# The same FFT and two MLP blocks with the engines' work listed in another order

## The chip, the cores and the metric

The kernel runs on one core of one Trainium2 chip. A core has five engines that work side by side, each through its own instructions in their order: TensorE (PE) does the matmuls, VectorE (DVE), ScalarE (ACT) and GpSimd (POOL) work elementwise, and SyncE (SP) issues most of the transfers. The metric is the device time of one execution in microseconds, as the median of several runs.

## The reference

The input x (2 batches of 3008 rows of 256) goes through three stages:

```python
X = np.fft.fft(x, axis=1)
X = np.fft.fft(X, axis=2)
x = X.real.reshape(6016, 256)
h = x @ w_in                                   # 256 -> 2048
x = (h * np.clip(h + 3.0, 0.0, 6.0) / 6.0) @ w_out
xn = x / np.sqrt(np.mean(x * x, -1, keepdims=True) + 1e-06) * rms_g
g = xn @ w_gate                                # 256 -> 1536
out = (g / (1.0 + np.exp(-g)) * (xn @ w_val)) @ w_out2
```

## The kernel before

All tensors of 32-bit numbers are split into a high and a low word that TensorE takes, so each product is three matmuls (high x high, high x low, low x high). The low word is made by a subtraction, `sub` at L271 to L272, on GpSimd or on VectorE. The weights come as 64-bit words and are decoded on the chip: `decode` (L254) is one ScalarE instruction (L260) and four of VectorE (L262, L263, L265, L267), then a copy for the high word and a `sub` for the low one.

The Fourier transform along the rows is done as matmuls with cosine and sine matrices (L439, from `smm`), after the input has been folded by symmetry (`sums`, `fold`). Its even and odd halves are added and subtracted into the arrays PQ and X (L456 to L461 and L469 to L478; the last three lines are copies of X by DMA). The transform along the 256 columns is multiplied into the first weights: `wmm` (L302) multiplies the columns' matrices by a quarter of w_in at L309, and splits the result at L318 and L320 into the array A0 to A3. One row of the product is copied out (L313), stored to memory as row0 to row3 (L315), and loaded again in another layout as c_wx (L322).

Phase 1 has 96 items, one for 1004 columns of tokens and 128 hidden channels (`item1`): six matmuls into the banks E and O (L536), a VectorE instruction that adds the x128 part by c_wx (L540), a sum and a difference (L542, L543), the activation (L548 on ScalarE, L551 on VectorE), the high word (L554), the low word (L272) and 12 matmuls into four acc banks (L570). E and O exist twice, so an item's first matmuls need that L551 two items back is done. Phase 2 has 144 items of 502 tokens (`item2`): 12 matmuls into E and O (L693), sigmoid (L696), two products (L699, L701), the high word (L705), the low word (L272), and six matmuls into two acc banks (L715). `rms` (L631) makes one normalized block of tokens from the results of phase 1, for 12 items each: a square on ScalarE, a sum over the channels by two matmuls (L649) into one of the E banks, a reciprocal square root in three rounds between ScalarE and VectorE (L654 to L664), a product (L667) and a split into words (L670, L672). `load_w2` and `conv_w2` bring and decode the weights of phase 2 while phase 1 runs.

What sets the order is a list written as a string, STEPS: 2554 words, each the name of a task in the table TASKS, a plain number for an item of phase 1, or a number with + for one of phase 2. Each word lets that task go on to its next `yield`, and everything it issues on the way is put at the end of the engines' queues:

```python
low[0] = V if step != task else G
```

A word with an apostrophe puts its subtraction L272 on VectorE, one without puts it on GpSimd. An engine does its instructions in that order alone; semaphores make it wait for what an instruction needs. So a step that stands early can hold up all that is queued behind it on each engine that it uses.

Of the kernel before, what the change touches and what calls it, by code (L numbers as in the profile page):

```python
# [83 lines left out]
    mat12 dwo0 PQ111 mat12 pq00' dwo0 PQ012 mat12 dwo0' ev01 PQ112 ev01 dwi1 lwo1 0 ev11 dwi1 ev11 dwi1 1 0 sx1 dwi1 sx1
    sx1 0 dwi1 X10 1 0 dwi1 1 X11 lwi2 0 1 X12 lwi3 lwo3 wt1 0 1 pq01 0 2 evx1 1 0 evx1 wt1 dwo1 2 1 2 0 wt1 1 wt1 wt1
    dwo1 2 evx1 pq01 dwi3 2 1 dwi3 2 wt1 wt1 2 lwo2 3 g wt1 wt1 2 3 4 dwi3 2 3 dwi3 3 4 3 4 5 3 dwo1 3 4 5 4 3 5 6 4 dwo1
    4 5 3 6 dwo1 5 4 6 7 5 dwo1 6 7 7 5 4 dwi2 6 5 dwi2 7 8 dwi2 6 5 7 6 dwi2 6 9 8 7 8 7 6 9 8 7 9 8 9 7 8 9 dwi2 8 10 9
    8 7 11 10 9 10 9 8 11 10 dwi2 11 10 11 9 dwo2 11 10 dwo2 10 wt2 11 dwo2 12 10 g wt2 12 11 12 10 wt2 dwi3 11 wt2 wt2
# [10 lines left out]
    45 pq10' 47 45 46 44 47 45 46 ls01 47 46 45 47 46 47 46 48 46 47 gr01 48 47 48 46 47 48 46 lm12 gr01 48 ls11 gr01 49
    48 48 47 49 49 48 ls11' 49 50 lw00 47 49 50 gr11 49 50 49 50 49 48 50 cw00 gr11 cw00 gr11 51 50 cw00 cw00 pq11 50 52  # L100
    51 lw10 cw00 lw01 51 50 49 52 51 cw00 52 51 52 50 51 52 51 53 52 51 54 53 52 53 51 52 54 53 54 53 54 52 53 54 rms2 53
    55 54 rms2 53 56 55 55 pq11 53 56 55 56 54 cw01 55 54 cw01 57 55 56 55 54 57 56 55 57 58 56 cw01 57 cw01 56 55 58 lw11
    cw01 57 56 cw01' 59 57 58 cw10 57 56 59 58 cw10 57 59 58 57 59 cw10 58 59 58 60 cw10 59 58 61 lw20 cw10 60 60 cw10 58
    61 60 59 cw10 61 cw11 59 60 59 61 cw11 60 cw11 61 60 62 cw11 61 60 lw21 cw11 63 62 62 61 60 63 cw11 62 63 61 cw20 cw11
    62 61 63 cw20 62 cw20 63 62 64 cw20 63 62 cw20 65 64 64 63 62 65 cw20 64 65 63 cw21 cw20 64 63 65 cw21 64 cw21 65 64
    66 63 cw21 64 67 66 65 66 64 cw21 65 67 66 67 65 rms0 66 cw21 65 67 66 cw21 67 66 rms0 68 67 66 69 68 68 67 66 69 67
    68 69 68 69 67 68 69 68 70 69 68 71 70 69 70 68 69 71 70 71 70 71 69 70 71 rms0 70 rms0 72 71 70 73 72 72 71 70 73 71
    72 73 72 73 71 72 73 72 rms0 73 74 72 rms0 75 rms0 73 74 rms0 72 74 73 75 74 rms0 75 73 rms0 75 74 rms0 75 74 76 pq12
    rms0 74 77 76 75 76 74 77 75 74 76 77 75 76 pq12 77 78 76 77 75 rms1 76 78 78 76 79 rms1 77 rms0 78 77 76 79 rms0 79
    77 78 79 77 rms0 78 79 78 rms0 80 79 78 rms0 81 79 80 78 81 79 80 81 80 79 rms0 81 80 lw30 rms0 81 80 82 rms0 79 80 83  # L110
    82 82 cw30 80 81 83 80 82 cw30 81 83 81 82 cw30 81 83 cw30 82 lw40 83 82 84 83 82 85 84 83 84 82 83 85 84 85 84 85 83
    84 85 84 86 85 84 87 86 85 86 84 cw30 85 87 86 cw30' 87 85 86 87 86 87 86 88 87 86 rms1 89 88 88 tw1 86 87 89 88 87 89
    88 89 87 88 89 88 rms1 90 89 88 91 90 90 tw2 88 89 91 90 89 91 90 91 89 90 91 90 rms1 91 92 90 rms1 93 rms1 91 92 90
    92 91 93 92 93 91 92 93 92 93 92 94 93 92 95 94 94 93 92 95 93 94 95 94 95 93 94 95 rms1 94 rms1 +0 95 94 rms1 95 94
    +0 rms1 +0 95 +0 rms1 +1 +0 rms1 +0 rms1 rms1 95 rms1 +1 rms1 rms1 +1 lw31 rms1 +2 +1 95 rms1 +1 +3 +2 +1 cw31 +2 cw31
    +2 +0 cw31 +2 +3 cw31 +2 +4 +3 lw41 cw31 +3 cw31 +3 +3 cw40 +5 +4 cw40 +4 cw40 +4 +1 +5 cw40 +4 +5 lw50 cw40 +6 +4 +5
    +5 cw40 +5 +2 +6 cw41 +6 +7 cw41 +6 cw41 +6 cw41 +6 +3 lw51 +7 cw41 +7 +4 cw41' +7 +8 +7 cw50 +7 cw50 +9 cw50 +8 cw50
    +8 lw60 cw50 +8 cw50 +5 +8 +9 +8 cw51 +9 +10 cw51 +9 cw51 +9 cw51 +9 +6 +10 lw61 cw51 +10 +11 cw51 +10 +10 cw60 +10
    cw60 +12 +11 cw60 +11 cw60 +11 +7 lw70 cw60 +11 cw60 +12 +8 +12 +11 cw61 +12 +13 cw61 +12 cw61 +12 cw61 +9 +13 +13
    lw71 cw61 +14 +13 cw61 +13 cw70 +13 cw70 +10 +14 rms2 cw70 +15 +14 cw70 +14 lw80 cw70 rms2 +14 cw70' +11 +14 +15 cw71  # L120
    +15 +12 cw71 +15 rms2 cw71 +15 +13 rms2 cw71 +15 lw81 cw71 +14 cw71' cw80 +16 cw80 cw80 cw80 cw80 +15 +16 cw80' +16
    +17 cw81 +16 cw81 +16 cw81 +16 cw81 +18 +17 +17 cw81 +17 +16 cw81' +17 +18 +17 +19 +18 +18 +18 +18 +17 +19 +19 +20 +19
    rms2 +19 +19 +21 +20 +20 rms2 +20 rms2 +20 +18 rms2 +21 +20 +21 rms2 +22 +21 rms2 +21 rms2 +21 rms2 +23 +22 rms2 +22
# [725 lines left out]
```

## Time and profile before

| | |
|---|---|
| median of 3 runs | 1104.33 us (1103.52 to 1104.47) |
| profiled execution | 1106.04 us |
| its span | 1104.1 us |
| mean granted TensorE clock | 0.992 |
| TensorE busy | 1056.1 us, 96%, 4572 matmuls |
| VectorE / ScalarE / GpSimd busy | 774.9 / 537.5 / 501.0 us |

The span runs from the first instruction to the last. The table by stage cuts it at places where the work changes: the transform up to about 60 us, its remainder mixed with the first items to about 142, phase 1 to about 500 (with the second batch's transform in it up to 366), then phase 2. Its busy times stand in the order PE, PEld (the loading of weights into TensorE), DVE, ACT, POOL. "Idle before <-" behind a timeline row is the time for which that engine had nothing to do, and what ended it.

### The profile page before, as it was taken

Reading aid. Unit: us, or ns where it says so; the run is one execution under the profiler, and the core shown is the slowest. Engines: PE = TensorE matmul, PEld = TensorE weight load, DVE = VectorE, ACT = ScalarE, POOL = GpSimd, SP = SyncE. Lnnn points to the kernel's source line nnn. Section 1 sums busy time; section 2 is a strip of 40 time slices with the busy share of each in tenths; the row PEclk is TensorE's granted clock in tenths of the full one; section 3 lists DMA queues with packets and bytes.
Section 4 is the critical chain, followed back from the end, with each engine's and each line's share of the span. In section 5 each row is a group of like instructions: output and inputs, shape, how many; then the busy total and the mean of one; then the engine's idle time right before and its main releaser. Section 6 shows DMA issues by size and latency. Waiting matters only on the chain.

```text
span 1104.1 us, 12691 instructions
## 1 busy us (share of the span) xinstructions
PE 1056.1 (96%) x4572; PEld 865.2 (78%) x4572; DVE 774.9 (70%) x1173; ACT 537.5 (49%) x814; POOL 501.0 (45%) x384
## 2 busy tenths in 40 slices
...
PEclk9899999999999999999999999999999999999999
...
GB/s 294 136 173 1 80 12 65 1 83 47 129 7 96 39 0 20 39 39 44 109 58 20 19 1 20 2 17 19 1 19 1 19 8 12 19 1 20 1 19 20
DMA packets 19175, 47.21 MB, mean 43 GB/s; under 512 B 3942, under 2 KB 7014, under 8 KB 18478
## 3 DMA queue, kind: packets, MB, share of 16 engines
...
## 4 chain that ended last, share of the span: by engine, by line
PE 67%; DVE 19%; POOL 5%; issue 3%; ACT 3%; DMA 2%; SPq 0%; DVEq 0%; ACTq 0%; POOLq 0%
PE acc L715 16%; PE E L693 16%; PE O L693 16%; PE acc L570 12%; POOL LO L272 4%; PE E L536 3%; PE O L536 3%; DVE R L551 3%; DVE T L540 2%; DVE O L543 2%; DVE E L542 2%; ACT HI L554 1%; PE E L439 1%; PE O L439 1%; DMA J<-in_x 1%
## 5 line engine op out<-in xcount | busy, mean ns | idle before, releaser
L272 POOL TENSOR_TENSOR LO<-R,HI 128x502 fp32r<-128x502 f32 x192 | 260.9, 1387 | 143.9 <-ACT HI L554 143.9
L570 PE MATMUL acc<-HI,B 128*128 128x502 f32 x768 | 248.4, 392 | 0.0
L699 DVE TENSOR_TENSOR R<-T,E 128x502 f32<-128x502 f32 x144 | 97.2, 675 | 201.1 <-ACT T L696 187.7
L272 POOL TENSOR_TENSOR HI<-R,HI 128x502 fp32r<-128x502 f32 x87 | 116.6, 1340 | 231.7 <-ACT HI L705 231.5
L570 PEld LDWEIGHTS acc<-HI,B 128*128 128x128 f32 x768 | 145.4, 189 | 30.6 <-POOL B L272 0.3
L570 PE MATMUL acc<-LO,B 128*128 128x502 f32 x384 | 151.2, 394 | 2.1 <-POOL LO L272 2.0
L693 PE MATMUL E<-J,B 128*128 128x502 f32 x576 | 147.9, 392 | 1.0 <-DVE R L699 1.0
L693 PE MATMUL O<-J,A 128*128 128x502 f32 x576 | 147.5, 391 | 1.1 <-DVE R L701 1.1
L272 POOL TENSOR_TENSOR LO<-R,LO 128x502 fp32r<-128x502 f32 x57 | 76.5, 1342 | 155.7 <-ACT LO L705 155.5
L554 ACT CAST HI<-R 128x1004 fp32r<-128x1004 f32 x96 | 99.0, 1033 | 66.2 <-PE acc L570 33.1
L696 ACT ACTIVATE T<-E 128x502 f32<-128x502 f32 x144 | 84.5, 588 | 94.4 <-PE E L693 94.2
L693 PEld LDWEIGHTS E<-J,B 128*128 128x128 f32 x576 | 108.6, 189 | 25.2 <-DVE R L699 2.6
L693 PEld LDWEIGHTS O<-J,A 128*128 128x128 f32 x576 | 108.9, 189 | 24.3 <-DVE R L701 1.5
L548 ACT ACTIVATE R<-E,c_three 128x502 f32<-128x502 f32 x96 | 65.4, 681 | 98.8 <-DVE E L542 65.4
L705 ACT CAST HI<-R 128x502 fp32r<-128x502 f32 x87 | 53.4, 613 | 112.3 <-DVE R L701 91.3
L701 DVE TENSOR_TENSOR R<-R,O 128x502 f32<-128x502 f32 x144 | 97.4, 676 | 11.7
L536 PE MATMUL E<-J,A 128*128 128x502 f32 x288 | 84.8, 403 | 14.6 <-DVE R L551 10.1
L715 PE MATMUL acc<-HI,B 128*128 128x502 f32 x354 | 89.7, 390 | 0.0
L570 PEld LDWEIGHTS acc<-LO,B 128*128 128x128 f32 x384 | 72.9, 190 | 19.9 <-POOL LO L272 4.9
L536 PE MATMUL O<-J,A 128*128 128x502 f32 x288 | 83.4, 399 | 0.8 <-DVE A L320 0.8
L536 PEld LDWEIGHTS E<-J,A 128*128 128x128 f32 x288 | 53.4, 192 | 33.3 <-DVE R L551 16.7
L715 PEld LDWEIGHTS acc<-HI,B 128*128 128x128 f32 x354 | 66.9, 189 | 14.0
...
## 6 DMA issues: line engine op xcount, KB each, us to landing
...
```

The lines of the kernel that those rows point to most:

```text
L272: low[0].tensor_tensor(o, a, b, op=ALU.subtract)
L536: T.matmul(bk[:, :BL], a[:, lw, eo, fs], j[:, eo, lx], start=(n == 0), stop=(n == 2))
L548: S.activation(x, bk[:, :BL], AF.Relu, bias=c3)
L551: V.scalar_tensor_tensor(x, x, 6.0, bk[:, :BL], op0=ALU.min, op1=ALU.mult)
L554: S.copy(hi, r)
L570: T.matmul(acc[k][:, :BL], w[:, lw, f % 4, d * P:(d + 1) * P], (hi, lo)[lx][:, hf * BL:(hf + 1) * BL], start=(first and n == 0), stop=(las ...
L693: T.matmul(bk[:, :BL], w[:, lw, d, fs], j[:, d, lx], start=(m == 0), stop=(m == 5))
L696: S.activation(s, E[:, :BL], AF.Sigmoid)
L699: V.tensor_tensor(u, s, E[:, :BL], op=ALU.mult)
L701: V.tensor_tensor(u, u, O[:, :BL], op=ALU.mult)
L705: S.copy(hl[0], u)
L715: T.matmul(acc[d][:, :BL], w[:, lw, f % 4, d * P:(d + 1) * P], hl[lx], start=(f == 0 and m == 0), stop=(f == NF2 - 1 and m == 2))
```

## The change

Only the string STEPS is changed. Each task has as many steps in it as before, the last 124 words are equal, and the matmuls are the same. Which low-word subtractions go to VectorE is changed too, since 21 words had an apostrophe and 20 have one now. The list's first lines and the one with the first step of item 24 of phase 2:

```diff
--- before.py
+++ after.py
@@ -76,93 +76,93 @@
     "x12": ("load_x", 1, 2, "PQ1", 1), "xq": ("load_xq",),
 }
 STEPS = """
-    one dm x01 x01 raw00 xq x00 x00 lwi0 raw01 raw02 x02 x02 raw11 raw10 fold1 fold1 fold1 fold1 fold1 mat00 mat00 fx
-    fold1 mat00 sx0 fold0 fold1 fold0 sx0 fold1' sx0 fold0 X00 fold1 fold0 fold1 fold0 dwi0 fold1' fold0 dwi0 fold0 mat01
-    fold0' mat01 dwi0 PQ100 mat01 mat02 fold0 dwi0 mat02 X01 fold0 fold2 lwi1 mat02 fold0' dwi0 PQ101 fold2 fold2 X02
...
-    rms2 +22 +19 rms2 +23 +22 rms2 +20 +22 +23 rms2 +23 rms3 rms2 +21 +23 +19 +19 +23 +24 +19 +19 +25 +24 +24 +24 +24 +26
...
+    one dm x01 x01 raw00 x00 x00 xq lwi0 raw02 raw01 x02 x02 raw11 raw10 fold1 fold1 fold1 fold1 fold1 mat00 mat00 fold1
+    mat00 fold0 fold1 fold0 fold1 fold1 fold0 fold1 fx fold0 sx0 fold0 sx0 dwi0 fold1' fold0 sx0 dwi0 fold0 X00 mat02
+    fold0' mat02 dwi0 mat02 PQ100 mat01 fold0 dwi0 mat01 PQ000 fold0 fold2 lwi1 mat01 fold0' X01 dwi0 fold2 PQ101 fold2
...
+    +22 rms2 +22 +19 rms2 +23 +22 rms2 +20 +22 +23 rms2 +23 +19 rms2 +21 +23 +19 rms3 +23 +19 +24 +19 rms3 rms3 rms3 +25
...
```

What this does to the queues is shown at three places. First SP's queue around the second set of X copies, some 50 to 70 us into the profile before. X1 and PQX0 hold the X piece, row1 and c_wx the small row of the second quarter of w_in, YB0, A2, A3, B0 and YB2 take 1 MB of raw weights each, c_g the gain of the norm. Before:

```order
L251 DMA YB0_70_374<-in_w_out 128x4x512
L251 DMA A2_84_434<-in_w_in 128x2x1024
L251 DMA A3_86_447<-in_w_in 128x2x1024
L251 DMA B0_87_449<-in_w_out 128x4x512
L315 DMA row1_62<-T0_105_513 1x512
L476 DMA X1_9_76<-PQX0_8_75 64x752
L477 DMA X1_9_76<-PQX0_8_75 64x752
L478 DMA PQX0_8_75<-PQX0_8_75 64x752
L251 DMA YB2_110_551<-in_w_out 128x4x512
L739 DMA c_g_3_70<-in_rms_g 128x2
L322 DMA c_wx_5_72<-row1_62 128x4x1
```

And now:

```order
L478 DMA PQX0_8_75<-PQX0_8_75 64x754
L251 DMA YB0_70_375<-in_w_out 128x4x512
L251 DMA A3_84_441<-in_w_in 128x2x1024
L476 DMA X1_9_76<-PQX0_8_75 64x752
L477 DMA X1_9_76<-PQX0_8_75 64x752
L478 DMA PQX0_8_75<-PQX0_8_75 64x752
L315 DMA row1_62<-T0_104_516 1x512
L251 DMA B0_106_540<-in_w_out 128x4x512
L251 DMA A2_107_544<-in_w_in 128x2x1024
L251 DMA YB2_108_546<-in_w_out 128x4x512
L322 DMA c_wx_5_72<-row1_62 128x4x1
```

The loads of A2 and B0 stood ahead of row1, and only that of YB2 between row1 and the load of c_wx from it; now all three stand there, and the copies of X have moved ahead of row1. Of the first set of X copies the opposite is true: before, the three copies (L476 to L478) stood ahead of row0 (L315), a load of matrices (L232) and the c_wx of row0 (L322); now these stand ahead of the three copies.

Second, VectorE's queue at items 11 and 12 of phase 1, some 111 to 123 us into the profile before. W1 and YB2 belong to the decode of a quarter of the weights, T0, E0, O0 and R0 to an item, A2 to the product of w_in with the columns' matrices. Before:

```order
L262 TENSOR_SCALAR W1_169_864<-W1_169_864 128x1024
L263 TENSOR_SCALAR W1_169_864<-W1_169_864 128x1024
L265 SCALAR_TENSOR_TENSOR W1_169_864<-YB2_110_551,W1_169_864 128x1024
L741 TENSOR_SCALAR c_gn_4_71<-c_g_3_70 128x2
L540 SCALAR_TENSOR_TENSOR T0_177_901<-PQX0_8_75,c_wx_5_72,E0_175_885 128x502
L542 TENSOR_TENSOR E0_175_885<-T0_177_901,O0_176_886 128x502
L543 TENSOR_TENSOR O0_176_886<-T0_177_901,O0_176_886 128x502
L272 TENSOR_TENSOR YB1_181_922<-W0_107_527,YB1_181_922 128x1024
L320 TENSOR_TENSOR A2_179_919<-E1_172_874,A2_179_919 128x512
L320 TENSOR_TENSOR A2_179_919<-O1_173_875,A2_179_919 128x512
L551 SCALAR_TENSOR_TENSOR R0_182_928<-R0_182_928,E0_175_885 128x502
L551 SCALAR_TENSOR_TENSOR R0_182_928<-R0_182_928,O0_176_886 128x502
```

And now:

```order
L741 TENSOR_SCALAR c_gn_4_71<-c_g_3_70 128x2
L262 TENSOR_SCALAR W1_171_870<-W1_171_870 128x1024
L263 TENSOR_SCALAR W1_171_870<-W1_171_870 128x1024
L540 SCALAR_TENSOR_TENSOR T0_178_902<-PQX0_8_75,c_wx_5_72,E0_175_886 128x502
L265 SCALAR_TENSOR_TENSOR W1_171_870<-YB2_108_546,W1_171_870 128x1024
L542 TENSOR_TENSOR E0_175_886<-T0_178_902,O0_176_887 128x502
L543 TENSOR_TENSOR O0_176_887<-T0_178_902,O0_176_887 128x502
L320 TENSOR_TENSOR A2_179_918<-E1_172_873,A2_179_918 128x512
L320 TENSOR_TENSOR A2_179_918<-O1_173_874,A2_179_918 128x512
L551 SCALAR_TENSOR_TENSOR R0_182_930<-R0_182_930,E0_175_886 128x502
L551 SCALAR_TENSOR_TENSOR R0_182_930<-R0_182_930,O0_176_887 128x502
```

The subtraction L272 of YB1 is gone from VectorE here (it is in GpSimd's queue), L741 has moved ahead of the decode, and L265 has moved behind an L540. A second L272, of B, is gone in the same way some ten rows later.

Third, TensorE's queue in phase 2 from the first matmul of item 24 on. E and O are the banks of an item's first matmuls, HI and LO the words that its output matmuls L715 read, J1 the normalized tokens. Before:

```order
L693 MATMUL E0_946_5022<-J1_943_5005,B0_483_2520 128x502 x6
L693 MATMUL O0_947_5023<-J1_943_5005,A0_740_3906 128x502 x6
L693 MATMUL E1_948_5038<-J1_943_5005,B0_483_2520 128x502 x6
L693 MATMUL O1_949_5039<-J1_943_5005,A0_740_3906 128x502 x6
L693 MATMUL E0_953_5059<-J1_943_5005,B0_483_2520 128x502 x6
L693 MATMUL O0_954_5060<-J1_943_5005,A0_740_3906 128x502 x6
L693 MATMUL E1_958_5082<-J1_943_5005,B0_483_2520 128x502 x6
L693 MATMUL O1_959_5083<-J1_943_5005,A0_740_3906 128x502 x6
L693 MATMUL E0_963_5104<-J1_943_5005,A1_727_3847 128x502 x6
L693 MATMUL O0_964_5105<-J1_943_5005,B4_826_4377 128x502 x6
L715 MATMUL acc2_839_4446<-HI2_941_4993,B3_902_4785 128x502 x3
L715 MATMUL acc3_840_4447<-HI2_941_4993,B3_902_4785 128x502 x3
```

And now:

```order
L693 MATMUL E0_946_5023<-J1_943_5005,B0_482_2518 128x502 x6
L693 MATMUL O0_947_5024<-J1_943_5005,A0_712_3768 128x502 x6
L693 MATMUL E1_949_5042<-J1_943_5005,B0_482_2518 128x502 x6
L693 MATMUL O1_950_5043<-J1_943_5005,A0_712_3768 128x502 x6
L649 MATMUL E0_954_5063<-LO2_948_5039,c_ones_1_68 128x502 x2
L715 MATMUL acc2_838_4445<-HI2_941_4993,B3_902_4791 128x502 x3
L715 MATMUL acc3_839_4446<-HI2_941_4993,B3_902_4791 128x502 x3
L715 MATMUL acc2_838_4445<-LO0_944_5016,B3_902_4791 128x502 x3
L715 MATMUL acc3_839_4446<-LO0_944_5016,B3_902_4791 128x502 x3
L715 MATMUL acc0_959_5088<-LO1_953_5061,B1_787_4187 128x502 x3
L715 MATMUL acc1_960_5089<-LO1_953_5061,B1_787_4187 128x502 x3
L693 MATMUL E1_961_5101<-J1_943_5005,B0_482_2518 128x502 x6
```

Before, the first matmuls of three more items stood between item 24's and the next L715; now the sum L649 of an rms block comes there, and L715 follows at once. Counted over the whole list, the output matmuls of items 22 to 52 stood 90 to 134 matmuls after the item's first one and now stand 38 to 84 after it; from item 65 on both are equal.

## Rows read from the trace of the kernel before

**Rows 1.** The page: busy time by engine, and the granted clock in 40 slices.
```profile
PE 1056.1 (96%) x4572; PEld 865.2 (78%) x4572; DVE 774.9 (70%) x1173; ACT 537.5 (49%) x814; POOL 501.0 (45%) x384
...
PEclk9899999999999999999999999999999999999999
```

**Rows 2.** Table by stage: stretch, its us, busy us (count) per engine, clock, DMA share, GB/s.
```profile
0.00:60.00 60.00, 34.13 (x138) 29.13 (x139) 47.41 (x90) 34.91 (x49) 3.29 (x6) 0.94 0.64 211
60.00:100.00 40.00, 35.10 (x138) 27.93 (x138) 36.95 (x52) 22.37 (x31) 27.38 (x18) 0.91 0.30 100
...
120.00:142.00 22.00, 19.13 (x74) 14.19 (x73) 21.55 (x31) 11.96 (x17) 10.46 (x10) 0.92 0.54 99
142.00:226.00 84.00, 80.42 (x348) 64.86 (x347) 80.76 (x130) 46.48 (x65) 62.00 (x45) 1.00 0.10 32
...
336.00:366.00 30.00, 28.90 (x124) 22.62 (x123) 28.82 (x48) 19.77 (x30) 20.96 (x16) 1.00 0.30 106
366.00:400.00 34.00, 34.00 (x150) 27.91 (x149) 28.98 (x45) 22.20 (x31) 25.08 (x20) 1.00 0.04 16
400.00:450.00 50.00, 46.66 (x199) 36.65 (x199) 48.72 (x73) 31.34 (x45) 31.59 (x23) 1.00 0.04 11
...
500.00:600.00 100.00, 97.98 (x425) 79.48 (x424) 76.12 (x115) 48.56 (x83) 42.04 (x31) 1.00 0.19 59
600.00:690.00 90.00, 90.00 (x395) 74.40 (x394) 53.70 (x76) 37.08 (x62) 28.73 (x22) 1.00 0.05 18
690.00:1100.00 410.00, 410.00 (x1796) 338.89 (x1794) 201.46 (x291) 152.73 (x252) 130.42 (x99) 1.00 0.03 11
```

**Rows 3.** Timeline at the start: start, us, engine, line, operation, idle before and releaser.
```profile
35.67 0.38 SPq L315 DMA_DIRECT2D row<-T  x1
...
36.90 0.69 DVE L263 TENSOR_SCALAR W<-W 128x1024 int32<-128x1024 int32 x1
...
37.74 0.47 ACT L456 COPY T<-O 128x377 f32<-128x377 f32 x1 [2.13 <-DMA row<-T]
...
39.41 0.65 PE L439 MATMUL E<-A,B 126*128 126x376 f32 x1 [4.60 <-DVE PQX L461]
```

**Rows 4.** Timeline 60 to 77 us: VectorE, the queue of SP, TensorE.
```profile
61.48 0.55 DVE L472 TENSOR_TENSOR PQX<-acc,T 128x376 f32<-128x376 f32 x1 [1.23 <-ACT T L469]
...
65.78 2.54 DVE L263 TENSOR_SCALAR W<-W 128x1024 int32<-128x1024 int32 x1
...
76.58 0.73 DVE L540 SCALAR_TENSOR_TENSOR T<-PQX,c_wx,E 128x502 f32<-128x502 f32 x1
...
70.33 0.41 SPq L322 DMA_DIRECT2D c_wx<-row  x1
...
71.48 0.96 PE L536 MATMUL E<-J,A 128*128 128x502 f32 x3 [2.97 <-DVE A L320]
```

**Rows 5.** VectorE from 111 to 126 us, and GpSimd's L272 (ns least/median/most).
```profile
111.90 0.69 DVE L262 TENSOR_SCALAR W<-W 128x1024 f32<-128x1024 f32 x1 [1.51 <-ACT W L260]
...
115.46 1.25 DVE L741 TENSOR_SCALAR c_gn<-c_g 128x2 f32<-128x2 f32 x1
...
118.63 1.60 DVE L272 TENSOR_TENSOR YB<-W,YB 128x1024 fp32r<-128x1024 f32 x1
...
125.74 1.66 DVE L272 TENSOR_TENSOR B<-W,B 128x1024 fp32r<-128x1024 f32 x1
...
L272 POOL TENSOR_TENSOR B<-W,B x3: 2390/2410/2418, 56.0 to 152.0; 128x1024 fp32r<-128x1024 f32 x3
```

**Rows 6.** TensorE near the end of phase 1.
```profile
444.80 0.94 PE L536 MATMUL E<-J,A 128*128 128x502 f32 x3 [0.86 <-DVE R L551]
```

**Rows 7.** TensorE at the start of phase 2.
```profile
514.64 1.62 PE L693 MATMUL O<-J,A 128*128 128x502 f32 x6 [1.05 <-DVE R L701]
```

**Rows 8.** Waits by pair: engine line <- engine line: us, times, longest us.
```profile
DVE R L654 <- ACT R L652: 15.8, 9, 1.9
...
DVE LO L662 <- ACT LO L660: 13.2, 19, 0.7
```

More of the change, by code (lines that the diff above doesn't have):

```diff
@@ L84 @@
[L84 to L88, printed above, removed]
@@ L99 @@
[L99 to L103, printed above, removed]
@@ L104 @@
[L104 to L123, printed above, removed]
@@ new lines @@
+    64 cw20 67 66 65 cw20 67 cw21 65 66 cw21 65 67 cw21 66 67 66 cw21 68 67 66 cw21 69 68 68 67 66 69 67 68 69 cw21 68 69
+    67 cw21 68 69 rms0 68 70 69 rms0 68 71 70 70 69 68 71 69 70 71 70 71 69 70 71 rms0 70 rms0 72 71 70 73 72 72 71 70 73
+    71 72 73 72 73 71 72 73 72 rms0 73 74 72 rms0 75 rms0 73 74 rms0 72 74 73 75 74 rms0 75 73 rms0 75 74 rms0 75 74 76
+    pq12 rms0 74 77 76 75 76 74 77 75 74 76 77 75 76 pq12 77 78 76 77 75 76 78 78 76 79 rms0 77 78 77 76 79 79 77 78 79 77
+    78 79 rms1 78 rms1 80 79 78 81 80 79 80 78 79 81 80 81 80 81 79 80 81 rms0 80 rms0 82 79 80 83 82 81 82 80 81 83 82 83
@@ new lines @@
+    81 82 81 83 82 83 82 rms0 84 83 82 rms0 85 83 82 84 85 83 84 tw1 85 84 83 85 84 85 84 86 rms0 84 85 87 86 lw30 86 84
+    87 85 84 86 87 85 cw30 86 87 cw30 88 cw30 86 87 85 86 88 cw30 86 88 lw40 cw30 89 87 cw30' 88 86 87 89 89 rms0 87 88 89
+    87 rms0 88 89 rms1 88 rms1 90 89 88 91 90 89 90 88 89 91 90 91 90 91 89 90 91 90 rms1 91 92 90 rms1 93 91 92 92 91 90
+    93 92 93 92 93 91 92 93 92 rms1 94 93 92 95 rms1 94 rms1 93 92 94 93 95 94 rms1 93 94 rms1 rms1 94 95 94 +0 rms1 95 94
+    rms1 95 tw2 94 +0 rms1 95 +0 rms1 95 +0 rms1 +1 +0 95 rms1 +0 95 +1 lw31 rms1 +1 +1 rms1 +2 +1 95 +1 cw31 +3 +2 cw31
@@ new lines @@
+    +2 cw31 +2 +0 +3 cw31 +2 +3 lw41 cw31 +4 +2 +3 +3 cw31 +3 cw40 +5 +4 cw40 +4 cw40 +1 +4 +5 cw40 +4 +5 +6 lw50 cw40 +4
+    +5 cw40' +5 cw41 +5 +2 +6 +6 +7 cw41 +6 cw41 +6 cw41 +6 +3 lw51 cw41 +7 cw41' +4 +7 cw50 +7 +8 cw50 +7 cw50 +7 cw50 +9
+    +8 lw60 cw50 +8 cw50' +8 cw51 +5 +8 cw51 +9 +8 cw51 +10 +9 cw51 +9 lw61 cw51 +6 +10 cw51 +9 +10 +11 +10 +9 cw60 +10
+    cw60 +10 cw60 +12 +11 +11 cw60 +11 lw70 cw60 +7 +12 cw60 +11 +12 +8 +12 +11 cw61 +12 cw61 +13 +12 cw61 cw61 +9 +13
+    lw71 cw61 +13 +14 cw61 +13 +13 cw70 +13 rms2 cw70 +15 +14 rms2 +14 cw70 +14 rms2 +15 cw70 +10 +14 +15 lw80 cw70 +14
```

102 lines of the change are left out of this document (57 added, 45 removed), and 13 rows, old and new, of the table STEPS.

## The prediction

> **What bounds the kernel now.** I read the busy times first, then the granted clock, a table by stage, the gaps that TensorE keeps, and what each of them waits for. TensorE is the bound: 1056.1 of the 1104.1 us span [rows 1]. From 690 us on it has no gap: 410 us for 1796 matmuls, 0.2283 us each [rows 2]. That pace is my yardstick: in any stretch, the time less its matmuls x 0.2283 is what the stage loses. By it 120 to 142 loses 22 - 74 x 0.2283 = 5.1 us, 142 to 226 loses 4.6, 336 to 366 1.7, 400 to 450 4.6, 500 to 600 3.0, while 366 to 400 and 600 to 690 lose nothing [rows 2]. The reader is to see in the same rows who sets these losses: VectorE is busy 21.55 of 22 us, 80.76 of 84, 28.82 of 30 and 48.72 of 50 in the losing stages, and 28.98 of 34 and 53.70 of 90 in those that lose nothing. In phase 1 a stage loses where VectorE is nearly full. The start has another bound: in the first 60 us the transfers run at 211 GB/s with the DMA engines busy 0.64 of the time [rows 2], and one gap of TensorE alone is 4.60 us [rows 3]. The clock is below full in the first 5 slices of 40 only [rows 1]; the mean of 0.92 in 120 to 142 [rows 2] means that about 16% of 22 us, 3.5 us, ran at the half level of 1.2 GHz, which is 1.8 of the 5.1 us lost there.
>
> **The change part by part.** The set of steps is the same and the matmuls are too, so nothing is won by less work on TensorE; a gain can only come out of the losses above, and a loss can come anywhere. From 690 us on both orders are so similar and the waits so few that I cost it at nothing. I sum against the profiled execution, 1106.04 us (span 1104.1 and 1.9 around it), which lies 1.71 us above the median of the runs, 1104.33; I assume that difference stays, so the sum is taken from the median.
>
> *0 to 60 us.* SP issued the copy of row0 (L315) at 35.67, behind three copies of X pieces; now it goes ahead of them. ScalarE waited 2.13 us for that copy until 37.74, and the copy and two VectorE adds behind it end TensorE's gap at 39.41 [rows 3]. But VectorE has a decode in the queue there, L262 and L263, the last from 36.90 for 0.69 us, to 37.59, while it took L459 up at 38.25 (0.47 of ScalarE and a handover after 37.74). So at most 38.25 - 37.59 = 0.66 us of the gap goes; what ends last then is L263. The X copies move behind the matrices' load, and are wanted later. First steps of other loads change places too. I take -0.7, bounds -2 (most of the wait) and +1.
>
> *60 to 100 us.* Two things. First, the second X piece (L472) made VectorE idle 1.23 us at 61.48 for ScalarE; it now comes earlier and TensorE's wait of 2.97 us at 71.48, which ends on VectorE's L320, could shrink [rows 4]. Against this, the order now puts one more decode instruction (L265) ahead of that L320, and an L540 that needs new matmuls between the two L320: I set that against the gain, -0.2 in all. Second, on SP the small load of c_wx row1 (L322) went out at 70.33 behind one load of 1 MB; now it stands behind three of 1 MB each. The L540 at 76.58 is the first that reads it [rows 4], and the L551 that frees the banks for the next matmuls is queued behind it on VectorE. I estimate that the three loads start some 4 us before the 70.33 of that row, at 66, because the X copies ahead of them come earlier. Their cost: at the mean of the first 60 us, 211 GB/s, 3.1 MB take 15 us, which lands c_wx at 81, 4.5 late; at 211 / 0.64 = 330 GB/s, engines always busy, 9.5 us and 75.5, in time. Back-to-back loads are nearer to the busy rate, so I take 1.2 us late. Sum +1.0, bounds -1.5 and +5.
>
> *100 to 142 us.* Two subtractions of weight words leave VectorE for GpSimd, 1.60 us at 118.63 and 1.66 at 125.74, and the negation L741 (1.25 us at 115.46) moves into the 1.51 us in which VectorE waited for ScalarE before 111.90 [rows 5]. That is 4.5 us off a VectorE that is busy 21.55 of 22. Another such subtraction (1.6 us by the same row) comes onto VectorE before 100 us, where it has 3 of 40 us free; it is within the bounds there. On GpSimd each takes 2.41 us [rows 5], and GpSimd has room, 10.46 of 22 busy [rows 2], but the subtractions of the items queue behind it: I charge 1.0. So -3.5 us, bounds -5.1 (the whole loss, half-level clock included) and -0.5.
>
> *142 to 226 us.* TensorE loses 4.6 with VectorE at 96%. The VectorE work per item is unchanged here; I cost it at nothing, by 1.0 either way, since backlog is carried through.
>
> *336 to 366 us.* One in three weight decodes (four VectorE instructions of 28.82 / 48 = 0.60 us) moves out to 366 to 400, where VectorE has 5.0 us free and TensorE does not wait [rows 2]. 2.4 us of relief could undo the whole 1.7; the stretched forms and GpSimd share it, so I take -1.2, bounds -1.7 and 0.
>
> *400 to 450 us.* Less rms and decode work stands ahead of the items from about 417 us on; it comes back in 450 to 470, where VectorE is less full. A wait like the 0.86 us at 444.80 on L551 [rows 6] can go; those up to 417 have the same queue ahead. Two thirds of the 4.6 us lie after 417 by length, 3.0; I take half, -1.5, bounds -3.5 and 0.
>
> *500 to 600 us.* The first gate weights' decode stood ahead of an item's L701 on VectorE, and TensorE waited 1.05 us for that L701 at 514.64 [rows 7]. The loads now go out earlier and rms1 is done ahead. Of the 3.0 lost, -1.2, bounds -2 and +1.
>
> *600 to 690 us.* Here the order takes back a cushion. Before, the output matmuls (L715) of item 24 of phase 2 stood 96 matmuls (21.9 us) after the item's first matmul; now 38 (8.7 us; the piece of the order shows the place). Counted from the order by mean durations, VectorE gets some 10 us more work in this stretch, 53.70 becomes about 64 of 90, and the three rms blocks lie in it. At VectorE 76.12 of 100 the stage 500 to 600 loses 3%, at 60% this one loses none [rows 2]: about 71% in between, so +1.0, bounds 0 and +8.
>
> Sum: -0.7 + 1.0 - 3.5 + 0 - 1.2 - 1.5 - 1.2 + 1.0 = -6.1. The median comes to 1104.33 - 6.1 = 1098.2 us. Adding up the likely side of each term gives 1092 to 1102 for this case.
>
> **The rivals.**
> *A, the relief is returned.* VectorE loses the subtractions, but waits come in their place: behind GpSimd's 2.41 us for the weight words, and VectorE's own instructions that work in SBUF alone stretch beside a busy GpSimd. For it: L263 took 2.54 us at 65.78 while the same form took 0.69 at 36.90 [rows 3, 4]. Against: most of VectorE's work in this stage reads PSUM, and GpSimd was 48% busy. Then the 100 to 142 term is 0, those of 336 to 366 and 400 to 450 are halved: -6.1 + 3.5 + 1.35 = -1.2, 1103.1 us.
> The Trainium skill, page "SBUF — State Buffer", section "Who interferes with whom", says that VectorE and GpSimd share a pair of ports as an exclusive lock, and that an instruction of VectorE with two SBUF inputs, or in a 2-port mode, is blocked for the whole of a GpSimd instruction that reads SBUF. The spread of L263 agrees with that. By the rule alone two subtractions of 2.41 us could block VectorE for 4.8 us and would cancel the 4.5 us taken off it; what no row shows is whether such instructions stand beside them in the new order.
>
> *B, the short cushion decides (slower).* With 8.7 us between an item's first matmul and its output, each of the three rms blocks between 600 and 690 us shows its chain: one wait of VectorE for ScalarE of 15.8 / 9 = 1.76 us and three of 13.2 / 19 = 0.69 [rows 8], 3.8 us, 11.5 for three. Then -6.1 - 1.0 + 11.5 = +4.4, 1108.7 us. It makes the kernel slower from (6.1 + 1.0 + 2.2) / 3 = 3.1 us per block on. For it: the bank in which the sum of squares is built is one of those that the items use. Against: the later stages run with a like cushion and with rms blocks in them, and lose nothing over 410 us.
>
> *C, all that VectorE costs from 100 us on is recovered.* 5.1 + 1.7 + 4.6 + 3.0 and the 0.7 of the start: -15.1, 1089.2 us. For it: each of these stages loses only where VectorE is full. Against: VectorE's total work is the same but for three subtractions, and what leaves one full stage must fit into the next.
>
> *D, it does not do what it says.* The waits follow whichever engine is behind, and the order of the matmuls is nearly the same: no change, 1104.
>
> **How the numbers follow.** The forecast's case has 0.60, A 0.15, B 0.12, C 0.07, D 0.06. 0.2% or 2.2 us is what can be told from no change. Of the forecast's case, 0.57 are beyond -2.2 and 0.03 within; C is faster; of A, 0.06 is faster, 0.08 the same, 0.01 slower; D is the same; of B, 0.11 is slower, 0.01 the same. Together faster 0.70, same 0.18, slower 0.12. The range takes in the forecast's own, A, D, and part of C: 1091 to 1105; B and the rest of C stay outside.
>
> **What would show it.** Right: in 120 to 142 us the changed kernel does more than 85 matmuls in 22 us or the same 74 in under 19; the long SBUF subtractions on GpSimd with no wait of VectorE or TensorE for them; no wait of 0.8 us on L551 near 440; the first gap of TensorE still 4 us. Wrong: a wait of VectorE's L540 for the transfer of c_wx at 76 to 80 us above 3 us; TensorE idle in 600 to 690; VectorE instructions stretched to 2 us beside GpSimd in 110 to 130. The prediction falls if the loss up to 142 us is not smaller, since more than half of the sum is made there.

## The result, and the profile after

The changed kernel takes 1111.88 us (median of 5 runs, 1111.28 to 1113.71) against 1104.47 us for the kernel before in 5 runs. The ratio is 1.0065, interval 1.0046 to 1.0084: it is 7.4 us slower. The forecast was 1098.2 us, 6.1 faster. The profiled execution of the changed kernel took 1113.33 us with a span of 1111.4.

First the page of the changed kernel, which answers to [rows 1]:

```profile
PE 1054.9 (95%) x4572; PEld 865.7 (78%) x4572; DVE 776.2 (70%) x1170; ACT 537.5 (48%) x814; POOL 507.2 (46%) x387
...
PEclk9889999999999899999999999999999999999999
```

The matmuls are the same, and so is the work of ScalarE; three subtractions net have gone from VectorE (1173 to 1170 instructions) to GpSimd (384 to 387). So nearly all of the difference is waiting (and some half clock). A new dip of the clock stands in the fourteenth slice. The table by stage of the changed kernel, against [rows 2]:

```profile
0.00:60.00 60.00, 32.73 (x139) 27.80 (x140) 47.86 (x89) 35.31 (x51) 5.06 (x7) 0.94 0.68 211
60.00:100.00 40.00, 32.41 (x128) 25.14 (x127) 36.23 (x49) 20.82 (x28) 24.20 (x16) 0.91 0.30 100
...
120.00:142.00 22.00, 18.98 (x78) 14.55 (x77) 20.14 (x29) 12.46 (x18) 14.12 (x11) 0.97 0.43 100
142.00:226.00 84.00, 78.77 (x335) 63.16 (x335) 80.47 (x128) 45.38 (x63) 61.70 (x44) 0.99 0.14 39
...
336.00:366.00 30.00, 29.58 (x130) 24.14 (x129) 27.49 (x44) 17.98 (x26) 20.77 (x16) 1.00 0.16 54
366.00:400.00 34.00, 28.98 (x116) 23.11 (x115) 28.02 (x42) 20.60 (x31) 20.16 (x16) 0.90 0.17 62
400.00:450.00 50.00, 47.77 (x207) 38.37 (x206) 43.99 (x67) 30.93 (x45) 32.55 (x24) 1.00 0.00 0
...
500.00:600.00 100.00, 98.30 (x428) 80.40 (x427) 78.95 (x117) 50.26 (x84) 41.46 (x31) 1.00 0.22 69
600.00:690.00 90.00, 90.00 (x396) 74.45 (x395) 61.44 (x90) 40.73 (x67) 28.09 (x21) 1.00 0.05 18
690.00:1100.00 410.00, 410.00 (x1796) 339.07 (x1795) 197.24 (x286) 151.11 (x251) 131.58 (x100) 1.00 0.03 11
```

The stage from 366 to 400 us is the one to look at: it did 150 matmuls and lost nothing, now it does 116 at a clock of 0.90. Since a shift in time moves work from window to window, I also set the start of the n-th matmul of one trace against that of the other. This is how far the changed kernel is behind at some of them (the times are those of before):

| matmul | at, us | behind, us | what lies between this row and the one above |
|---|---|---|---|
| 160 | 65 | -0.1 | start |
| 260 | 97 | +2.3 | waits at 72 to 92 us |
| 680 | 202 | +2.2 | nothing, within a microsecond |
| 1280 | 336 | +4.2 | two waits near 210 us, less 0.6 |
| 1380 | 361 | +2.5 | a gain |
| 1440 | 375 | +10.7 | the wait at 376.55 us and half clock behind it |
| 1680 | 432 | +11.7 | a small loss |
| 1760 | 453 | +8.8 | a gain |
| 2100 | 534 | +6.4 | a gain |
| 2260 | 570 | +8.7 | one wait of 1.46 us at 567.87, and smaller ones |
| last | 1100 | +7.3 | a gain of 1.0 to 590, then nothing |

The greatest step, on the timeline of the changed kernel around 370 us (columns as in [rows 3]; SPq is SP's queue of transfers, c_p a weight being decoded; x2 is two instructions in one row, with the time of the first):

```profile
363.01 1.30 POOL L272 TENSOR_TENSOR LO<-c_p,LO 128x512 fp32r<-128x512 f32 x1
...
368.52 1.12 DVE L267 SCALAR_TENSOR_TENSOR c_p<-W,c_p 128x512 int32<-128x512 int32 x1
...
369.71 0.38 SPq L599 DMA_DIRECT2D W<-in_w_out  x1
...
370.18 7.33 SPq L623 DMA_DIRECT2D scratch<-LO  x2
...
374.95 0.62 ACT L618 CAST LO<-c_p 128x512 fp32r<-128x512 f32 x1 [5.29 <-DMA scratch<-LO]
375.47 1.02 ACT L554 CAST HI<-R 128x1004 fp32r<-128x1004 f32 x1
...
376.55 0.79 PE L570 MATMUL acc<-HI,B 128*128 128x502 f32 x1 [4.12 <-ACT HI L554]
```

Read it from the bottom. TensorE waits 4.12 us for an item's high word (L554). ScalarE makes it late because the instruction ahead of it, a weight's high word (L618), waited 5.29 us until the buffer LO2 was stored to memory. GpSimd had finished the words to be stored at 364.3, but SP issued the store (L623) at 370.18 only: ahead of it in SP's queue stood a load (L599, into W1) that had to wait until 369.7 for its buffer. The last instruction that reads this buffer is L267 of the decode cw20, from 368.52 for 1.12 us, to 369.64; it stands behind that load in the list of steps. The same store and L618 in the kernel before, where the store went out as soon as GpSimd was done (361.5) and ScalarE did not wait:

```profile
360.23 1.30 POOL L272 TENSOR_TENSOR LO<-c_p,LO 128x512 fp32r<-128x512 f32 x1
...
361.56 10.70 SPq L623 DMA_DIRECT2D scratch<-LO  x2
...
367.67 0.67 ACT L618 CAST LO<-c_p 128x512 fp32r<-128x512 f32 x1
```

### The profile page after: what moved, and what is told of

The parts are those of the page before. It is cut to its first block, busy times and chain, and to the rows that moved or that the text cites. A ratio compares the mean times of both kernels' runs of the same rounds, so it can differ in the third digit from the quotient of the medians.

```text
span 1111.4 us, 12685 instructions
## 1 busy us (share of the span) xinstructions
PE 1054.9 (95%) x4572; PEld 865.7 (78%) x4572; DVE 776.2 (70%) x1170; ACT 537.5 (48%) x814; POOL 507.2 (46%) x387
## 4 chain that ended last, share of the span: by engine, by line
PE 72%; DVE 18%; issue 3%; POOL 2%; ACT 2%; DMA 2%; SPq 0%; DVEq 0%; ACTq 0%; POOLq 0%
PE acc L715 17%; PE O L693 16%; PE E L693 16%; PE acc L570 14%; PE E L536 4%; PE O L536 3%; DVE R L551 3%; DVE T L540 2%; DVE O L543 2%; DVE E L542 2%; POOL LO L272 2%; DMA J<-in_x 1%; PE E L439 1%; PE O L439 1%; DVE c_p L267 1%
## 5 line engine op out<-in xcount | busy, mean ns | idle before, releaser
L272 POOL TENSOR_TENSOR LO<-R,HI 128x502 fp32r<-128x502 f32 x192 | 263.4, 1399 | 141.7 <-ACT HI L554 138.7
L272 POOL TENSOR_TENSOR HI<-R,HI 128x502 fp32r<-128x502 f32 x87 | 116.4, 1338 | 241.5 <-ACT HI L705 241.5
L272 POOL TENSOR_TENSOR LO<-R,LO 128x502 fp32r<-128x502 f32 x57 | 75.2, 1319 | 146.3 <-ACT LO L705 146.1
L554 ACT CAST HI<-R 128x1004 fp32r<-128x1004 f32 x96 | 99.2, 1033 | 75.5 <-DVE R L551 40.1
L715 PE MATMUL acc<-HI,B 128*128 128x502 f32 x354 | 89.8, 390 | 0.0
L715 PEld LDWEIGHTS acc<-HI,B 128*128 128x128 f32 x354 | 66.9, 189 | 14.0
```

The costliest lines, as they stand in the source:

```text
L272: low[0].tensor_tensor(o, a, b, op=ALU.subtract)
L554: S.copy(hi, r)
L715: T.matmul(acc[d][:, :BL], w[:, lw, f % 4, d * P:(d + 1) * P], hl[lx], start=(f == 0 and m == 0), stop=(f == NF2 - 1 and m == 2))
```

## The experiments

Each of the twelve kernels was timed in 5 rounds against the kernel before. Ratios are to that kernel, with their 95% intervals; the changed kernel has 1.0065. Every kernel is one of the two lists of steps with words put in another order, or the front of one list and the end of the other.

| run | what it is | ratio | interval |
|---|---|---|---|
| e1 | changed, lw11 ahead of lw20 | 1.0002 | 0.9991 to 1.0012 |
| e2 | before, lw20 ahead of lw11 | 1.0055 | 1.0035 to 1.0076 |
| e3 | changed, 50 to 85 us as before | 1.0050 | 1.0035 to 1.0065 |
| e4 | changed, 85 to 175 us as before | 1.0062 | 1.0044 to 1.0080 |
| e5 | changed, fold steps as before | 1.0046 | 1.0031 to 1.0062 |
| e6 | before to 345 us, then changed without the exchange | 0.9978 | 0.9967 to 0.9989 |
| e7 | changed, 13 words near 70 us | 1.0033 | 1.0020 to 1.0045 |
| e8 | before to 400 us, then changed | 0.9977 | 0.9965 to 0.9990 |
| e11 | changed with e1, e5 and e7 | 0.9966 | 0.9953 to 0.9979 |
| e12 | e11, rms2 as before | 0.9952 | 0.9935 to 0.9969 |
| e13 | e11, a decode moved into idle time | 0.9971 | 0.9957 to 0.9985 |
| e14 | before, two subtractions to GpSimd | 0.9994 | 0.9980 to 1.0008 |

**The exchange of two loads (e1, e2).** lw20 and lw11 start loads of half a megabyte of weights. Their buffers are given out in turn, W0 and W1 (`rr("W", 2)`). The change put lw20 ahead of lw11, so the two swapped buffers, and the next load, lw21, got the buffer of the decode cw20 instead of that of cw11, which is done earlier. e1 takes that back in the changed kernel:

```diff
-... 60 lw20 lw11 60 59 ...
+... 60 lw11 lw20 60 59 ...
```

> The changed kernel with two words exchanged: lw11 stands ahead of lw20 again, as before the change. Nothing else differs. The two loads take the buffers W0 and W1 in turn, so the exchange gives the third load, lw21, the buffer that the decode cw11 has already left, instead of the one that the decode cw20 still reads. Theory 1 (a store queued on SP behind a stalled load): the store of the low and high words to memory goes out at about 364 us instead of 370.18, ScalarE's wait of 5.29 us for it and TensorE's of 4.12 us at 376.55 go, with the stretch of half clock behind them; of the 7.9 us that the changed kernel loses between 366 and 376 us at least 7 come back: 1104 to 1105 us, a ratio to before of 1.000. Theory 2 (the store is late for another reason, the transfers or GpSimd): the wait stays, 1111 to 1112 us. Theory 3 (the time comes back as a wait on another engine soon after, since phase 1 is bound by VectorE): half of it, about 1108 us.

e2 makes the same exchange in the kernel before:

```diff
-... 58 lw11 cw01 57 ... 61 lw20 cw10 60 ...
+... 58 lw20 cw01 57 ... 61 lw11 cw10 60 ...
```

> The kernel before with the same two words exchanged: lw20 ahead of lw11. Theory 1 (the store behind a stalled load): the third load now waits on SP for a buffer that a later decode still reads, the store behind it is late by about 6 us, and TensorE shows a new wait of about 4 us between 360 and 375 us with half clock behind it: 1111 to 1112 us, a ratio of 1.006 to 1.007. Theory 2 (other reasons): within 1 us of before. Theory 3: about 1108 us.

Both come out as theory 1 has it: 1.0065 goes to 1.0002 by the exchange of two words, and 1 to 1.0055 by the same exchange the other way round. In e1, the last reader of the load's buffer (L267), SP's queue, the words to be stored, and ScalarE:

```profile
359.35 1.23 DVE L267 SCALAR_TENSOR_TENSOR c_p<-W,c_p 128x512 int32<-128x512 int32 x1
...
360.64 0.38 SPq L599 DMA_DIRECT2D W<-in_w_out  x1
...
362.90 1.29 POOL L272 TENSOR_TENSOR LO<-c_p,LO 128x512 fp32r<-128x512 f32 x1
...
364.21 8.25 SPq L623 DMA_DIRECT2D scratch<-LO  x2
...
369.56 0.62 ACT L618 CAST LO<-c_p 128x512 fp32r<-128x512 f32 x1
```

The load goes out at 360.64, when L267 (here of cw11) is done, the store behind it at 364.21, when GpSimd is done, and L618 has no wait. In e2 the same chain appears where it was not:

```profile
355.79 1.29 POOL L272 TENSOR_TENSOR LO<-c_p,LO 128x512 fp32r<-128x512 f32 x1
...
361.66 0.73 DVE L267 SCALAR_TENSOR_TENSOR c_p<-W,c_p 128x512 int32<-128x512 int32 x1
...
362.45 0.38 SPq L599 DMA_DIRECT2D W<-in_w_out  x1
362.92 7.34 SPq L623 DMA_DIRECT2D scratch<-LO  x2
...
367.76 0.62 ACT L618 CAST LO<-c_p 128x512 fp32r<-128x512 f32 x1 [4.89 <-DMA scratch<-LO]
...
370.98 0.79 PE L570 MATMUL acc<-LO,B 128*128 128x502 f32 x1 [3.81 <-POOL LO L272]
```

The words to be stored were ready at 357.08 and went out at 362.92, behind the load that L267 released at 362.39. ScalarE waits 4.89 us for the store and TensorE 3.81, here by way of GpSimd, where the item's low word stood behind a weight's, which waits for L618. The exchange is worth 0.0063 or some 7 us by the one pair of ratios and 6 by the other: nearly the whole of the slowdown.

**The steps near 70 us (e3, e7).** The changed kernel there, VectorE and then TensorE, against [rows 4]:

```profile
66.06 2.64 DVE L262 TENSOR_SCALAR W<-W 128x1024 f32<-128x1024 f32 x1
...
70.52 1.22 DVE L265 SCALAR_TENSOR_TENSOR W<-A,W 128x1024 int32<-128x1024 int32 x1
71.66 0.68 DVE L320 TENSOR_TENSOR A<-E,A 128x512 fp32r<-128x512 f32 x1
74.06 0.74 DVE L540 SCALAR_TENSOR_TENSOR T<-PQX,c_wx,E 128x502 f32<-128x502 f32 x1 [1.72 <-PE E L536]
74.71 0.69 DVE L320 TENSOR_TENSOR A<-O,A 128x512 fp32r<-128x512 f32 x1
...
72.40 1.62 PE L536 MATMUL E<-J,A 128*128 128x502 f32 x3 [3.99 <-DVE A L320]
...
75.45 0.79 PE L536 MATMUL O<-J,A 128*128 128x502 f32 x1 [1.43 <-DVE A L320]
```

TensorE's E matmuls start when the first L320 has freed the bank, L540 needs their result, and the second L320, which frees the bank for the O matmuls, is queued behind that L540. So TensorE and VectorE wait for each other in turn. e3 takes the whole stretch back, e7 only these 13 words:

```diff
-dwi3 2 3 wt1 2 wt1 3 wt1 2 wt1 3 4 dwi3
+2 wt1 2 wt1 wt1 wt1 3 2 dwi3 3 4 3 dwi3
```

> The changed kernel with the 124 words from fold2's fourth step to item 3's fourth (about 50 to 85 us) as they were before the change. Theory 1 (one more decode instruction ahead of the first L320 and an L540 between the two make TensorE wait 4.0 and 1.4 us at 72 and 75 us, where it waited 3.0 once): TensorE's pattern of before returns there, 2.0 to 2.5 us less than the changed kernel, 1109.5 us, ratio 1.0045. Theory 2 (the loss there is made up by the loss at 137 us that follows, because VectorE's queue sets the pace from 100 to 142 us): 1111 to 1112 us.

> The changed kernel with 13 words put in another order around 70 us: the decode instruction L265 and item 3's L540 stand behind both L320 instead of ahead of them and between them; all else, the stores' order too, as in the changed kernel. Theory 1 (that L265, 1.22 us, and the L540 that needs TensorE's result make up the loss at 72 to 76 us): TensorE's waits of 4.0 and 1.4 us there become one of 2.8, 2.0 us less or, with a shorter stretch at half clock, up to 3: ratio about 1.0045. Theory 2 (the decode instructions L262 that are stretched to 2.64 us beside GpSimd make it up): the first wait stays above 3.5 us and less than 1 us is gained, ratio 1.006.

e7 gains 0.0032, 3.5 us, somewhat more than theory 1's; but both ratios have their intervals, and by matmuls counted (the start of its n-th matmul set against that of the changed kernel, as in the table of matmuls) its trace wins 2.1 us between 65 and 97 us, as theory 1 has it. Its TensorE waits once for 2.87 and once for 0.77 us:

```profile
69.69 0.95 PE L536 MATMUL E<-J,A 128*128 128x502 f32 x3 [2.87 <-DVE A L320]
71.42 1.62 PE L536 MATMUL O<-J,A 128*128 128x502 f32 x3 [0.77 <-DVE A L320]
```

In the changed kernel these are 3.99 and 1.43. e3 gains 0.0015 with an interval that overlaps that of the changed kernel; it agrees with theory 1 but shows little by itself. By matmuls counted its trace wins 2.5 us there and loses 1.1 of them again near 140 us, where its clock is lower (0.86 over 120 to 142 us against 0.97).

**The relief of VectorE from 110 to 130 us (e4, e14, e13).** My prediction's greatest term was 3.5 us for two subtractions taken off VectorE and a third instruction moved into its idle time. e4 puts the stretch back into the changed kernel; e14 takes just two subtractions off VectorE in the kernel before:

```diff
-wt2 wt2 dwi3' 12 wt2 ... dwo2' wt3 13
+wt2 wt2 dwi3 12 wt2 ... dwo2 wt3 13
```

> The changed kernel with the 131 words from item 5's first step to dwo3's second (about 85 to 175 us) as they were before the change: two subtractions of weight words are on VectorE again and one is on GpSimd again. Theory 1 (the relief of VectorE there was worth nothing, since VectorE then waits 0.45 and 1.04 us for TensorE and ScalarE at 125 to 128 us, and what sets TensorE's waits at 138 us is the queue of VectorE after that): the same within 1 us, 1111 to 1112 us; with the 1 us wait of TensorE for the subtraction that came onto VectorE at 92 us gone, 1110.5. Theory 2 (my prediction's term: the relief is worth 3.5 us and something else hid it): 1115 us.

> The kernel before with two apostrophes taken away: the last subtractions of dwi3 and dwo2 (1.60 us at 118.63 and 1.66 at 125.74 on VectorE) go to GpSimd, and nothing is moved. My prediction's term by itself: these 3.3 us off VectorE give 2.5 to 3.5 us, ratio 0.997. Theory 1 (VectorE then waits for TensorE and ScalarE instead, the wait at 137 us stays): within 1 us of before, with a wait of VectorE for ScalarE's L318 of about 1 us near 127 us. Theory 2 (VectorE is blocked beside GpSimd's 2.4 us): slower by 1 us or more, with instructions of VectorE stretched there.

Neither changes the time within its interval: 1.0062 against 1.0065, and 0.9994 against 1. The 1115 us (1.0097) of theory 2 in e4 and the 0.997 of my term in e14 lie outside their intervals. By matmuls counted the relief is worth 0.3 us up to 136 us in e14 and 0.7 in e4. e14 shows where 3.26 us of VectorE's work went, on VectorE and TensorE:

```profile
118.80 0.69 DVE L320 TENSOR_TENSOR A<-O,A 128x512 fp32r<-128x512 f32 x1 [0.70 <-ACT A L318]
...
122.50 0.74 DVE L540 SCALAR_TENSOR_TENSOR T<-PQX,c_wx,E 128x502 f32<-128x502 f32 x1 [0.70 <-PE E L536]
...
125.65 0.69 DVE L320 TENSOR_TENSOR A<-E,A 128x512 fp32r<-128x512 f32 x1 [1.04 <-ACT A L318]
...
135.26 1.27 PE L536 MATMUL E<-J,A 128*128 128x502 f32 x3 [1.98 <-DVE R L551]
```

2.44 of the 3.26 us are now waits of VectorE, which had none between 112 and 130 us before, the last and longest for a copy of TensorE's matmuls L309. From 125.65 on the order is as before, and TensorE's wait behind it is 1.98 us, where the kernel before has 1.93 at 136.81. VectorE was busy nearly all the time before and yet a lighter load did not help: at 125.65 it meets TensorE's result in any case. e13 tries to use the idle time, by a decode put into it:

```diff
-wt3 13 wt3 dwo2 wt3 13 wt3 14 13 wt3 dwo3 x10
+wt3 dwo3 13 wt3 dwo2 wt3 13 wt3 14 13 wt3 x10
```

> The kernel with the three repairs, and in addition one word moved: the decode instructions L262 and L263 of dwo3 (1.07 and 1.65 us at 131 us) go into VectorE's idle place before the L320 of A3, where it waited 1.04 us for ScalarE's L318. Theory 1 (between 128 and 142 us TensorE's wait is set by what stands in VectorE's queue behind that handover, and the relief ahead of it ran idle): the waits of 2.07 and 0.68 us at 138 us shrink by about 1 us and the stretch at half clock may go too, 1 to 2.7 us less. Theory 2 (VectorE is full up to 226 us anyway): less than 0.5 us.

It gains nothing over e11 (0.9971 against 0.9966): TensorE's wait of 1.93 us at 136.53 in e11 is gone, but one of 2.26 us at 129.09 has come, where e11 has 0.27. The decode instruction met GpSimd's subtraction there:

```profile
124.87 3.57 DVE L263 TENSOR_SCALAR W<-W 128x1024 int32<-128x1024 int32 x1
128.36 0.68 DVE L320 TENSOR_TENSOR A<-E,A 128x512 fp32r<-128x512 f32 x1
...
125.48 2.40 POOL L272 TENSOR_TENSOR B<-W,B 128x1024 fp32r<-128x1024 f32 x1
```

L263 took 3.57 us where it takes 0.69 alone [rows 3], and ended 0.56 us after the subtraction's end at 127.88. The Trainium skill, page "SBUF — State Buffer", section "Who interferes with whom", has VectorE and GpSimd share a pair of ports, which the one that issues first keeps for its whole instruction while the other is blocked. The run agrees in that L263 ended only behind the subtraction; but by the records L263 began 0.61 us ahead of it and yet gave way, which the run does not explain.

**The fold's steps at 210 us (e5).** In the changed kernel three L347 (and a fourth of 0.41 us) stand ahead of the L551 that TensorE waits for:

```profile
210.54 3.23 DVE L347 TENSOR_TENSOR W<-W 126x256 f32<-126x256 f32 x3
...
214.88 0.95 PE L536 MATMUL E<-J,A 128*128 128x502 f32 x3 [1.57 <-DVE R L551]
```

e5 puts the 46 words back, of which these matter:

```diff
-lf2 30 29 28 31 30 29 31 32 30 lf2 30 31 29 lf2 30 ...
+30 29 28 31 31 29 30 31 29 30 31 30 lf2 32 30 31 33 32 ...
```

> The changed kernel with the 46 words from item 30's fourth step to lm01 (about 205 to 225 us) as they were before the change: the last three steps of the second batch's fold (L341 and L347) stand later again, behind the L551 of items 29 to 31. Theory 1 (these VectorE instructions, 1.65 us and three of 3.23 us together, stood ahead of the L551 that TensorE waits for, 0.46 and 1.57 us at 209 and 215 us): both waits go, 1.9 us less than the changed kernel, ratio about 1.0048. Theory 2 (VectorE is full there, 96%, so what is taken away at 210 us is lost again by 226): the same as the changed kernel, 1.0065.

1.0046, 0.0019 or 2.1 us less, the number of theory 1; by the times alone the two intervals overlap. The trace speaks for theory 1: the waits of 0.46 and 1.57 us are not there, and by matmuls counted the run wins 2.5 us there, gives 0.6 back by 230 us and keeps the rest up to 360 us.

**What the change won (e8, e6).** e8 is the list before up to word 934 and the changed list from there; e6 changes over at word 789 and has the loads in the old order.

```diff
 e8: before[:934] + after[934:]
 e6: before[:789] + after[789:], with lw11 ahead of lw20
```

> The kernel before up to the 934th word (about 400 us), the changed one from there on: phase 1's end with less work of the rms blocks ahead of its items, the earlier loads at the start of phase 2, and the shorter distance from an item's first matmul to its output. My prediction put -1.5 (400 to 450 us), -1.2 (500 to 600) and +1.0 (600 to 690) on these. Theory 1 (these terms hold; the two traces give -2.0, -1.9 and +0.9 less 0.3 by matmuls counted): 1101 us, ratio 0.997. Theory 2 (the waits of phase 1's end only come back at another item, since VectorE is 97% busy from 400 to 450): ratio 1.000. Theory 3 (the short distance costs): 1.002 or more.

> The kernel before up to the 789th word (about 345 us), the changed one from there on, with lw11 ahead of lw20. Left out are all changes in the first 345 us and the exchange of the two loads. Theory 1 (the losses of the change are the exchange, the steps around 70 us and the fold steps at 210 us; what is left of it are gains of 1.4 us at 345 to 365 and 3.4 from 400 us on): 1099.5 us, ratio 0.9955, faster than both. Theory 2 (the gain at 345 to 365 us goes with the exchange of the loads): 1101 us, 0.997. Theory 3 (one state of VectorE's queue replaces another): 1104 us, 1.000.

The late part is a real gain, 0.0023 or 2.5 us (1102.35 us), less than the 3.4 that I expected: in its trace the wait of [rows 6] is gone and so is that of [rows 7]; one at L649 is there, 1.40 us. e6 has the same time, so the 1.4 us gained from 345 to 365 us did not come through. The ratio is nearest to theory 2's, but its reason does not hold: without the exchange e6's trace wins 1.7 us by 361 us and loses 2.5 again by 414, since TensorE has new waits of 0.61 us at 368 and 0.64 at 398 us, and one of 0.95 at 406 where the kernel before has 0.37. For this part one state replaced another, as in theory 3.

**All repairs together (e11, e12).** e11 is the changed list with the edits of e1, e5 and e7; e12 has also the steps of the third rms block at 550 to 570 us as before, because of this wait in the changed kernel:

```profile
567.87 0.72 PE L649 MATMUL E<-LO,c_ones 128*128 128x502 f32 x2 [1.46 <-DVE R L699]
```

```diff
-rms2 cw70 +15 +14 rms2 +14 cw70 +14 rms2 ...
+cw70 +10 +14 rms2 cw70 +15 +14 cw70 +14 ...
```

> The changed kernel with the three repairs at once: lw11 ahead of lw20, L265 and item 3's L540 behind both L320, and the fold's last steps back behind the L551. If the three losses are separate, the ratios add up: 1.0065 - 0.0063 - 0.0032 - 0.0019 = 0.9951, about 1099 us, faster than both kernels. If one replaces another (VectorE's queue hands what is won at 70 or 210 us to the next full stage): 0.998 or more.

> The kernel with the three repairs, and in addition the 35 words from cw70's second step to item 16's first of phase 2 (about 550 to 570 us) as before the change: the third rms block's steps, L649 with it, stand later. Theory 1 (L649 came too early and waited 1.4 us for the bank that L699 frees): that wait goes, 0.7 to 1.5 us less than with the three repairs alone. Theory 2 (VectorE's work there is only put off): the same as with the three repairs.

e11 takes 1101.17 us, ratio 0.9966 (0.9953 to 0.9979): faster than both kernels. The sum of the single ratios, 0.9951, lies just outside that interval, and e11 is below the 0.998 of the other case. Of the 0.0114 that the three won singly it has 0.0099; each of the three has an uncertainty of its own of some 0.002, so whether a small part is lost between them stays open. In e12 the wait at L649 is gone, and its ratio is 0.9952, but the medians are 1101.09 and 1101.17 and the intervals overlap: whether that wait was worth anything is not settled.

## Why the prediction was wrong

The sign was wrong because of one mechanism that no term of the sum and none of the rivals had: a store queued on SP behind a load that has no buffer yet. It cost 7 of the 7.4 us. Without it (e1) the change is worth nothing (1.0002), and not the 6.1 us of the forecast: the relief of VectorE did not pay, and there are losses near 70 and 210 us. Step by step, by the table of matmuls:

- *0 to 60 us*, -0.7 predicted, none measured (0.1); the start varies by more than that in these traces (e7, with the order of the changed kernel up to there, is 1.6 us ahead of it at 65 us).
- *60 to 100 us*, +1.0 predicted, +2.3 measured, with the cause at the other place. The late c_wx did not matter: the L540 that reads it first was reached at 79.43 us and had no wait. The L265 ahead of L320, and the L540 between the two, which I had set against a gain and called -0.2, cost it: by moving these alone e7 gets 2.1 us back by matmuls counted, 3.5 by the ratios. The wait of VectorE for TensorE's new matmuls at 74.06 and of TensorE for VectorE at 75.45 could have been read from the order, since each needs the other's result.
- *100 to 142 us*, -3.5 predicted, 0 measured within the intervals (e4, e14), at most 0.7 us by matmuls counted. This was the largest term, and the step that failed in it is "4.5 us off a VectorE that is busy 21.55 of 22": a busy share near 1 does not make an engine the bound if it meets another engine's result at a fixed point. Of rival A, "the relief is returned", this part came true, mostly as waits, and with stretched instructions too (L262 took 1.83 us at 114.59 in the changed kernel, 0.69 in the one before [rows 5]).
- *142 to 226 us*, 0 predicted "by 1.0 either way", +1.9 measured: I had said that VectorE's work per item is unchanged there and had not looked at the fold's last steps, the last three of which the change had brought forward by 12, 21 and 29 words (e5).
- *336 to 366 us*, -1.2 predicted, -1.7 measured by the table. e1 and e6 show that it is not kept: both lose 2.5 us again by 414 us.
- *366 to 400 us*: I had moved work into it because TensorE does not wait there [rows 2]. The failed step is that I counted a decode's VectorE instructions and not its load and store: the exchange of lw20 and lw11 was in the list, but no term follows SP's queue behind 120 us, or the turn in which the two buffers are given out (e1, e2).
- *400 to 450*, -1.5 predicted, -1.9 measured; *500 to 600*, -1.2 predicted, -0.9 measured (2.1 gained near 515 us, 2.2 lost from 534 to 570, the wait at L649 in it, and 1.0 gained behind). e8 shows 2.5 us for both, against 2.7 predicted.
- *600 to 690 us*, +1.0 predicted, none lost. Rival B, the short cushion, did not happen: VectorE is at 61.44 of 90 us and TensorE has no gap. Its sign, slower, came true for another reason.

One of the signs of being wrong that were named in advance did come: the loss up to 142 us is not smaller. Three workings were off besides, and none of them decides the result. A nine in [rows 1] means 0.9 or more, so that row does not show where the clock is full; the last stretch at the half level before phase 2 lies at 137.6 to 141.0 us, nearly all of it in the sixth slice. The sum of rival C leaves out the 4.6 us of 142 to 226; with them it is -19.7. And the interpolation for 600 to 690 us gives 1.9, where 1.0 was taken.
